# Moving a layout copy from VectorE to GpSimd, and logarithms ahead of sums, in a fused attention and feed-forward kernel

## Chip, cores and metric

The kernel runs on one core of one Trainium2 chip. The metric is the device time of one execution in microseconds (us), as a median of several runs. Engines are called by their names in the profile: PE (matmul), PEld (weight load), DVE (VectorE), ACT (ScalarE), POOL (GpSimd), SP (SyncE, which here only issues transfers). All times inside an execution count from the start of its span. L510 is line 510 of a kernel; the same line has other numbers in other kernels. A transfer *lands* when its data have arrived. The *granted clock* is the share of the full PE clock that the profile shows as granted. A run over 1.5% above the fastest of its kernel counts as slow, and ratios use fast runs alone.

## The reference, cut to what matters

```python
# q, k, v: 8 batches x 8 heads x 576 x 64;  s: 8 x 8 x 576;  all float32
scores = q @ k.transpose(0, 1, 3, 2) / sqrt(64)
cum    = cumsum(maximum(s, 0), axis=-1)
scores = where(causal, -1e9, scores + minimum(-(cum_i - cum_j), 0))   # (cut)
attn   = softmax(scores) ;  y = attn @ v
x      = y as 4608 tokens x 512
out    = gelu(x @ w_in) @ w_out        # w_in 512 x 2048, w_out 2048 x 512
```

The additive bias depends on the key through `cum_j`, so the kernel multiplies v and a row of ones by a weight per key (`wb`) instead of adding it to the scores. Attention is then, for each pair of heads, a numerator (P times weighted v) and a denominator (P times weights), and the quotient is formed as numerator times exp(−ln(denominator)).

## The kernel before

Tokens are worked in nine chunks of 512; chunk c runs the two feed-forward layers of its tokens on PE while the attention of batch c+1 is woven between them. Batch 0's attention is the prologue: nothing runs beside it. A batch has four pairs of heads, each with scores, an exponential (ACT), two mask products (DVE), the numerator and denominator (PE), a logarithm and an exponential (ACT) and the quotient `xT` (DVE). From batch 2 on, q and k are loaded with two heads apart, interleaved on chip (`interleave`), written to DRAM as rows and read back by transposing transfers. These are the pieces that the change touches:

```python
def interleave(b, n):                          # L176
    i = 0 if n == "q" else 1
    t = qk_of[b, i] = work.tile([128, 2, G, 2, D], bf16, tag="qkbf", bufs=2, name="qk_bf")
    for j in range(2):
        nc.vector.tensor_copy(                 # L180, DVE
            t[:, j].rearrange("g r e d -> g e r d"),
            early[b, n][:, j].rearrange("g e (r d) -> g e r d", r=G))

def av_banks(wide=False, last=False):          # PSUM for numerator and denominator
    if wide:
        t = ps.tile([128, 2, 512], fp32, tag="sc", bufs=2, name="avw")
        return t[:, 0], t[:, 1]                # both sums in ONE tile
    # ... otherwise two tiles, avn and avd

def av_item(b, p, wide=False, rest=True):
    num, den = av_banks(wide)
    av_mm(b, p, num, MAIN, False)              # L425, numerator first
    av_mm(b, p, den, MAIN, True)               # L425, then denominator
    if rest:
        av_rest(b, p)
    norm(b, p, p + 1, num, den, 0, CUT, [...]) # L442 ln, L443 exp (ACT), L458 xT (DVE)

# end of chunk 0, batch 1's attention between pieces of the second layer (cut)
            scale_pair(1, 2)                   # L232: v times weights, DVE
            av_item(1, 0, rest=False)
            scale_pair(1, 3)
            l2_item(c, 3, 8, 12)
            av_item(1, 1, wide=True, rest=False)
            interleave(2, "q")
            write_rows(2, 0, nc.sync)
            av_item(1, 2, wide=True, rest=False)
            l2_item(c, 3, 12)
            interleave(2, "k")
            write_rows(2, 1, nc.sync)
            av_item(1, 3, rest=False)
            # ... transposes of batch 2, loads of batch 3
```

## Time and profile before

| | before |
|---|---|
| median of 3 runs | 333.96 us (333.59 to 335.59) |
| profiled run | 333.42 us, span 331.6 us |
| PE busy | 317.4 us, 96% of the span |
| DVE, ACT, POOL busy | 191.3, 204.1, 66.0 us |
| chain that ended last | PE 81%, DMA 8%, ACT 4%, DVE 3% |
| prologue, chunks 0, 1, 2, 3 | 24.23, 38.32, 35.44, 35.21, 34.05 us |

PE is nearly always busy, so a change in another engine can only matter where PE stands still. The lines that show where it does stand in the prediction below, with how to read their columns.

### The profile page before, as it was taken

Reading aid. Unit: us, or ns where it says so; the run is one execution under the profiler, and the core shown is the slowest. Engines: PE = TensorE matmul, PEld = TensorE weight load, DVE = VectorE, ACT = ScalarE, POOL = GpSimd, SP = SyncE. Lnnn points to the kernel's source line nnn. Section 1 sums busy time; section 2 is a strip of 40 time slices with the busy share of each in tenths; the row PEclk is TensorE's granted clock in tenths of the full one; section 3 lists DMA queues with packets and bytes.
Section 4 is the critical chain, followed back from the end, with each engine's and each line's share of the span. In section 5 each row is a group of like instructions: output and inputs, shape, how many; then the busy total and the mean of one; then the engine's idle time right before and its main releaser. Section 6 shows DMA issues by size and latency. Waiting matters only on the chain.

```text
span 331.6 us, 8751 instructions
## 1 busy us (share of the span) xinstructions
PE 317.4 (96%) x3760; PEld 193.4 (58%) x3762; DVE 191.3 (58%) x382; ACT 204.1 (62%) x290; POOL 66.0 (20%) x100
## 2 busy tenths in 40 slices
PE   8879999999999999999999999999999999999992
PEld 3456645666666556656665566656665666555562
DVE  4659428997369464866577557845693764150021
ACT  3677656869567774767676777586768676204400
POOL 8754342002500370440035001300000000000000
PEclk9999999999999999999999999999999999999997
DMA  7999999564995699999759977625610110010012
GB/s 115 222 211 210 218 198 275 200 95 69 220 311 88 103 247 258 190 194 194 251 131 206 235 194 118 153 99 166 119 34 33 43 57 2 34 63 34 1 65 71
DMA packets 53838, 47.45 MB, mean 143 GB/s; under 512 B 31329, under 2 KB 43873, under 8 KB 53793
## 3 DMA queue, kind: packets, MB, share of 16 engines
q0 software_dynamic: 15936, 23.07, 38.0%
q1 hardware_dynamic: 37856, 23.75, 28.6%
q8 instruction: 31, 0.51, 0.6%
q14 instruction: 15, 0.11, 0.1%
HBM read 36.85 MB, written 16.52 MB: 161 GB/s over the span
## 4 chain that ended last, share of the span: by engine, by line
PE 81%; DMA 8%; ACT 4%; DVE 3%; issue 2%; POOL 1%; SPq 0%; DVEq 0%; POOLq 0%
PE h_ps L510 36%; PE o_ps L532 31%; DMA early_q<-in_q_dram 4%; PE sc_ps L387 4%; PE avd L425 3%; PE avn L425 3%; ACT P L403 2%; DMA qkT<-rows 2%; DVE xT L458 1%; PE o_ps L553 1%; DMA early_q<-in_k_dram 1%; PE tr_ps L366 1%; PE avr L425 1%; DVE qkT L372 1%; PE warm L582 1%
## 5 line engine op out<-in xcount | busy, mean ns | idle before, releaser
L532 PE MATMUL o_ps<-w_out_r,gT 128*64 128x512 bf16 x1120 | 129.8, 380 | 0.0
L510 PE MATMUL h_ps<-xT,w_in_r 128*64 128x512 bf16 x1152 | 126.4, 379 | 2.5 <-DVE xT L458 2.5
L510 PEld LDWEIGHTS <-w_in_r 128*64 128x64 bf16 x1152 | 76.5, 110 | 50.4 <-issue 3.3
L532 PEld LDWEIGHTS <-gT 128*64 128x64 bf16 x1120 | 62.7, 110 | 48.3
L517 ACT ACTIVATE gT<-h_ps 128x1024 bf16<-128x1024 f32 x54 | 54.3, 1022 | 49.9 <-PE h_ps L510 49.9
L403 ACT ACTIVATE P<-sc_ps 128x1024 bf16<-128x1024 f32 x64 | 62.0, 1021 | 30.8 <-PE sc_ps L387 27.2
L539 DVE COPY o_sb<-o_ps 128x512 f32<-128x512 f32 x35 | 24.0, 686 | 47.9 <-PE o_ps L532 47.9
L412 DVE TENSOR_TENSOR P<-P,tri_bf 128x512 bf16<-128x512 bf16 x58 | 24.0, 422 | 38.3 <-ACT P L403 38.0
L215 DVE TENSOR_REDUCE amx<-qkT 128x2 f32<-128x1152 bf16 x32 | 40.9, 1336 | 0.0
L204 POOL DMA_DIRECT2D raw_v<-in_v_dram x40 | 34.2, 879 | 9.5 <-DMA w_out_r<-in_moe_w_out_dram 4.8
L458 DVE SCALAR_TENSOR_TENSOR xT<-avn,ln 128x256 bf16<-128x256 f32 (+3 forms) x64 | 21.6, 384 | 22.3 <-ACT ln L443 22.2
L232 DVE TENSOR_TENSOR vv<-raw_v,wb 128x512 bf16<-128x512 f32 (+3 forms) x44 | 25.2, 632 | 0.0
L442 ACT ACTIVATE ln<-avd 128x256 f32<-128x256 f32 x56 | 18.6, 392 | 10.2 <-PE avd L425 10.2
L443 ACT ACTIVATE ln<-ln 128x512 f32<-128x512 f32 (+1 forms) x40 | 23.5, 588 | 1.3
L520 ACT ACTIVATE gT<-h_ps 128x512 bf16<-128x512 f32 x36 | 19.6, 603 | 6.3 <-PE h_ps L510 6.3
L387 PE MATMUL sc_ps<-qkT 64*128 64x256 bf16 (+2 forms) x320 | 21.1, 250 | 2.1 <-ACT P L403 1.0
L222 DVE TENSOR_REDUCE amv<-raw_v 128x1 f32<-128x2048 f32 (+1 forms) x16 | 22.9, 1470 | 0.0
L387 PEld LDWEIGHTS <-qkT 64*128 64x128 bf16 x320 | 12.9, 94 | 16.8 <-issue 12.2
L425 PEld LDWEIGHTS <-vv 128*64 128x64 bf16 x384 | 18.0, 110 | 4.9 <-PE sc_ps L387 0.9
L425 PEld LDWEIGHTS <-wb 128*64 128x64 bf16 x384 | 17.7, 111 | 1.8 <-issue 1.7
L425 PE MATMUL avd<-P,wb 128*64 128x256 bf16 x224 | 15.6, 260 | 1.0 <-DVE xT L458 1.0
L425 PE MATMUL avn<-P,vv 128*64 128x256 bf16 x224 | 15.8, 263 | 0.6 <-DVE P L412 0.6
(98 smaller groups left out, 156.9 us busy)
## 6 DMA issues: line engine op xcount, KB each, us to landing
out_dram<-o_sb SPq DMA_DIRECT2D x35, 256.0 KB, 3.2
raw_v<-in_v_dram POOLq DMA_DIRECT2D x32, 256.0 KB, 8.1
rows<-qk_bf SPq DMA_DIRECT2D x12, 576.0 KB, 6.1
early_q<-in_q_dram POOLq DMA_DIRECT2D x13, 288.0 KB, 10.6
early_k<-in_k_dram POOLq DMA_DIRECT2D x13, 288.0 KB, 11.7
w_in_r<-in_moe_w_in_dram POOLq DMA_DIRECT2D x4, 512.0 KB, 11.4
w_out_r<-in_moe_w_out_dram POOLq DMA_DIRECT2D x4, 512.0 KB, 14.3
raw_v<-in_v_dram POOLq DMA_DIRECT2D x8, 128.0 KB, 9.1
```

The costliest lines, as they stand in the source:

```text
L204: nc.gpsimd.dma_start(out=t[:n_st, st, :, :], in_=bass.AP(tensor=v.tensor, offset=v.offset + b * H * S * D + st * 128 * D, ap=[[D, n_st], ...
L215: nc.vector.tensor_reduce(amx[:, b * NP + p], qkT[b % 2][:, :, p, :S], axis=AX, op=ALU.max, apply_absolute_value=True)
L232: eng.tensor_tensor(vb[:n_st, st0:st1, h0:h1, :], t[:n_st, st0:st1, h0:h1, :], wb[:n_st, st0:st1, b * H + h0 : b * H + h1] .unsqueeze(3).t ...
L387: nc.tensor.matmul(s_ps[:, e, off : off + n], lhsT=qkT[b % 2][e * 64 : e * 64 + 64, 1, p, jt * 128 : jt * 128 + 128], rhs=qkT[b % 2][e * 6 ...
L403: nc.scalar.activation(P[:, :, UO[u] : UO[u] + UW[u]], s_ps[:, :, : UW[u]], func=AF.Exp, scale=scale)
L412: eng.tensor_tensor(d, d, tri_bf.unsqueeze(1).unsqueeze(1).to_broadcast([128, 2, 2, 128]), op=MULT)
L425: nc.tensor.matmul(out[e * 64 : e * 64 + 64, lo : lo + n], lhsT=(wb[:, jt, b * H + h : b * H + h + 1].to_broadcast([128, 64]) if den else ...
L458: nc.vector.scalar_tensor_tensor(out if p1 - p0 > 1 else out[:, 0], cut(num), math.exp(-LNC[c]), cut(ln), op0=MULT, op1=MULT,)
L510: nc.tensor.matmul(h_of[c, f2][i][e * 64 : e * 64 + 64], lhsT=w_in_r[:, ko, ft * 128 + e * 64 : ft * 128 + e * 64 + 64], rhs=xT[:, ko, c * ...
L517: nc.scalar.activation(gT_of[c][:, f2 * 2 : f2 * 2 + 2, :], hh_of[c, f2], func=AF.Gelu)
L532: nc.tensor.matmul(o_ps[e * 64 : e * 64 + 64], lhsT=gT[:, ft, t0 : t0 + 64], rhs=w_out_r[:, ft, :], start=(ft == 0), stop=(ft == FT - 1), ...
L539: nc.vector.tensor_copy(o_sb, o_ps)
```

## The change

Its intent is to shorten the places where PE waits: batch 0's scores are transposed and computed in the order in which the loads land (Part 1), the denominators and their logarithms come ahead of the numerators everywhere (Part 2), the end of chunk 0 is reordered and two copies move from DVE to ACT (Part 3), and the interleave goes from DVE to POOL for all batches (Part 4). The diff, cut to its core:

```diff
@@ interleave
-            nc.vector.tensor_copy(
+            nc.gpsimd.tensor_copy(
@@ norm is split: norm_act = ln and exp on ACT, norm_dve = the quotient on DVE
@@ av_item
     num, den = av_banks(wide)
+    av_mm(b, p, den, MAIN, True)
+    ln = norm_act(den, CUT, CHUNKS)
     av_mm(b, p, num, MAIN, False)
-    av_mm(b, p, den, MAIN, True)
     ...
-    norm(b, p, p + 1, num, den, 0, CUT, [(0, 0, 256), (1, 256, CUT)])
+    norm_dve(b, p, p + 1, num, ln, 0, CUT, CHUNKS)
@@ prologue (cut)
-    tr_items(0, 1, (0, 1))
-    weights_dve()
-    keep_busy(5)
+    keep_busy(1)
+    tr_items(0, 1, (0,))
+    keep_busy(2)
+    tr_items(0, 1, (1,))
+    keep_busy(3)
     sc_item(0, 1, neg=True, units=(0,))
     ...
+    lns = {p: norm_act(avs[p][1], CUT, CHUNKS) for p in (0, 1)}
     for p in range(NP):
         av_mm(0, p, avs[p][0], MAIN, False)
-        norm(0, p, p + 1, *avs[p], 0, CUT, [(0, 0, 256), (1, 256, CUT)])
+        norm_dve(0, p, p + 1, avs[p][0], lns[p], 0, CUT, CHUNKS)
+        if p + 2 < NP:
+            lns[p + 2] = norm_act(avs[p + 2][1], CUT, CHUNKS)
@@ chunk 0, after its first layer
             load_v(2)
+            interleave(2, "q")
+            interleave(2, "k")
@@ end of chunk 0 (cut)
+            av_item(1, 0, rest=False)
+            scale_pair(1, 2)
             l2_item(c, 3, 4, 8)
             sc_item(1, 3)
-            scale_pair(1, 2)
-            av_item(1, 0, rest=False)
+            av_item(1, 1, rest=False)
             scale_pair(1, 3)
+            write_rows(2, 0, nc.sync)
             l2_item(c, 3, 8, 12)
-            av_item(1, 1, wide=True, rest=False)
-            interleave(2, "q")
-            write_rows(2, 0, nc.sync)
             av_item(1, 2, wide=True, rest=False)
+            write_rows(2, 1, nc.sync)
             l2_item(c, 3, 12)
-            interleave(2, "k")
-            write_rows(2, 1, nc.sync)
             av_item(1, 3, rest=False)
```

More of the change, by code (lines that the diff above doesn't have):

```diff
@@ L436, with norm_act @@
     rest_of = {}
-    def norm(b, p0, p1, num, den, i0, i1, chunks):
+    def norm_act(den, w, chunks):
         ln = work.tile([128, CUT], fp32, tag="ln", bufs=2, name="ln")
-        w = (p1 - p0) * (i1 - i0)
         for c, lo, hi in chunks:
@@ L443, in norm, with norm_dve @@
         nc.scalar.activation(ln[:, :w], ln[:, :w], func=AF.Exp, scale=-1.0)
+        return ln
+    def norm_dve(b, p0, p1, num, ln, i0, i1, chunks):
+        w = (p1 - p0) * (i1 - i0)
         for c, lo, hi in chunks:
@@ L470, in av_banks @@
             return num, den
-        return [ps.tile([128, 512], fp32, tag="av", bufs=3, name=n) for n in ("avn", "avd")]
+        den, num = [ps.tile([128, 512], fp32, tag="av", bufs=3, name=n) for n in ("avd", "avn")]
+        return num, den
+    CHUNKS = [(0, 0, 256), (1, 256, CUT)]
     def av_item(b, p, wide=False, rest=True):
         num, den = av_banks(wide)
+        av_mm(b, p, den, MAIN, True)
+        ln = norm_act(den, CUT, CHUNKS)
         av_mm(b, p, num, MAIN, False)
-        av_mm(b, p, den, MAIN, True)
         if rest:
             av_rest(b, p)
-        norm(b, p, p + 1, num, den, 0, CUT, [(0, 0, 256), (1, 256, CUT)])
+        norm_dve(b, p, p + 1, num, ln, 0, CUT, CHUNKS)
     def av_rest(b, p):
@@ L488, in norm_rest @@
         t = rest_of[b].rearrange("d n p i -> d n (p i)")
-        norm(b, 0, NP, t[:, 0], t[:, 1], CUT, S, [(2, 0, NP * SL)])
+        chunks = [(2, 0, NP * SL)]
+        ln = norm_act(t[:, 1], NP * SL, chunks)
+        norm_dve(b, 0, NP, t[:, 0], ln, CUT, S, chunks)
     gT_of = {}
@@ L520, in l1_item, with l2_item @@
                 nc.scalar.activation(gT_of[c][:, f2 * 2 + i, :], h_of[c, f2][i], func=AF.Gelu)
-    def l2_item(c, sub, f0=0, f1=FT, av=False):
+    def l2_item(c, sub, f0=0, f1=FT, av=False, copy=None):
         gT = gT_of[c]
@@ L538, in l2_item @@
         o_sb = work.tile([128, KO * 128], fp32, tag="osb", bufs=3, name="o_sb")
-        nc.vector.tensor_copy(o_sb, o_ps)
+        (copy or nc.vector.tensor_copy)(o_sb, o_ps)
         r0 = c * NB + sub * 128
@@ L589 @@
     nc.vector.tensor_scalar(neg_bf, tri_bf, 2048.0, -2048.0, op0=MULT, op1=ALU.add)
+    keep_busy(1)
+    tr_items(0, 1, (0,))
+    keep_busy(2)
+    tr_items(0, 1, (1,))
     keep_busy(3)
-    tr_items(0, 1, (0, 1))
-    weights_dve()
-    keep_busy(5)
     sc_item(0, 1, neg=True, units=(0,))
     tr_items(0, 2, (0,))
+    keep_busy(1)
+    tr_items(0, 2, (1,))
+    weights_dve()
     sc_item(0, 1, neg=True, units=(1,))
+    tr_items(0, 3, (0,))
+    sc_item(0, 2, neg=True, units=(0,))
     weights_pe()
-    tr_items(0, 2, (1,))
+    tr_items(0, 3, (1,))
+    sc_item(0, 2, neg=True, units=(1,))
     mask_item(0, 0, 0, nc.vector)
-    tr_items(0, 3, (0,))
-    keep_busy(1)
-    sc_item(0, 2, neg=True)
-    tr_items(0, 3, (1,))
     mask_item(0, 0, 1, nc.vector)
@@ L671 @@
             l2_item(c, 1, 8, 12, av=True)
-            l2_item(c, 2, 0, 12, av=True)
-            l2_item(c, 0, 12)
+            l2_item(c, 2, 0, 8, av=True)
+            l2_item(c, 0, 12, copy=nc.scalar.copy)
+            l2_item(c, 1, 12, av=True)
             tr_items(1, 2, (0, 1), (nc.scalar.copy, nc.vector.tensor_copy), wide=True)
-            l2_item(c, 1, 12, av=True)
-            tr_items(1, 3, (0, 1), (nc.scalar.copy, nc.vector.tensor_copy), wide=True)
+            l2_item(c, 2, 8, 12, av=True)
+            tr_items(1, 3, (0, 1), (nc.scalar.copy, nc.scalar.copy), wide=True)
+            scale_pair(1, 0)
             l2_item(c, 2, 12, av=True)
-            scale_pair(1, 0)
+            scale_pair(1, 1)
             l2_item(c, 3, 0, 4)
             sc_item(1, 2)
-            scale_pair(1, 1)
+            av_item(1, 0, rest=False)
+            scale_pair(1, 2)
             l2_item(c, 3, 4, 8)
             sc_item(1, 3)
-            scale_pair(1, 2)
-            av_item(1, 0, rest=False)
+            av_item(1, 1, rest=False)
             scale_pair(1, 3)
+            write_rows(2, 0, nc.sync)
             l2_item(c, 3, 8, 12)
-            av_item(1, 1, wide=True, rest=False)
-            interleave(2, "q")
-            write_rows(2, 0, nc.sync)
             av_item(1, 2, wide=True, rest=False)
+            write_rows(2, 1, nc.sync)
             l2_item(c, 3, 12)
-            interleave(2, "k")
-            write_rows(2, 1, nc.sync)
             av_item(1, 3, rest=False)
```

## The prediction

> **What bounds the kernel now.** I read the page first: PE is busy 317.4 of 331.6 us and carries 81% of the chain that ended last. The question is therefore only where PE stands still and which of those places the change reaches. The busy times by stretch answer it. I cut at the first matmul of each chunk's first layer (L510) as the timeline gives it; the columns are length, busy time of PE, PEld, DVE, ACT and POOL (with instruction counts), granted clock, DMA share, GB/s.
>
> ```profile
> 0.00:24.23 24.23, 19.06 (x294) 10.88 (x296) 13.80 (x32) 14.11 (x22) 17.59 (x32) 1.00 1.04 180
> 24.23:62.55 38.32, 36.76 (x538) 22.57 (x538) 25.74 (x49) 27.23 (x41) 12.96 (x17) 1.00 1.06 207
> 62.55:97.99 35.44, 34.69 (x422) 22.80 (x423) 25.21 (x47) 23.81 (x35) 6.92 (x10) 1.00 0.84 190
> 97.99:133.20 35.21, 34.42 (x395) 21.82 (x392) 22.00 (x41) 24.05 (x35) 9.68 (x15) 1.00 0.87 179
> 133.20:167.25 34.05, 34.05 (x395) 20.69 (x392) 22.08 (x40) 23.95 (x35) 7.11 (x10) 1.00 1.04 201
> ```
>
> From 133.2 us on PE has no idle time (34.05 of 34.05; the next three stretches and the last full chunk are alike). No rearrangement of work on other engines can shorten these 200 us; it can only spoil them. The recoverable time lies in the prologue (24.23 us, of which 7.4 us are filler matmuls, L582), in chunk 0 (1.56 us idle), chunk 1 (0.75) and chunk 2 (0.79). The DMA share is about 1 up to 62 us: loads land when the queue gets to them, however early the compute is.
>
> The waits of PE, then the timeline, tell which work ends these gaps (start, length, instruction; in brackets the idle time before it and what ended it):
>
> ```profile
> PE h_ps L510 <- DVE xT L458: 2.5, 3, 1.1
> PE avd L425 <- DVE xT L458: 1.0, 2, 0.5
> PE avn L425 <- DVE P L412: 0.6, 2, 0.3
> ```
>
> ```profile
> 11.28 2.13 ACT L403 ACTIVATE P<-sc_ps 128x1024 bf16<-128x1024 f32 x2 [1.68 <-PE sc_ps L395]
> 14.81 1.94 ACT L403 ACTIVATE P<-sc_ps 128x1024 bf16<-128x1024 f32 x2 [1.03 <-PE sc_ps L395]
> 17.50 1.94 ACT L403 ACTIVATE P<-sc_ps 128x1024 bf16<-128x1024 f32 x2 [0.75 <-PE sc_ps L395]
> 20.86 0.66 ACT L442 ACTIVATE ln<-avw 128x256 f32<-128x256 f32 x2 [1.43 <-PE avw L425]
> 22.21 0.76 DVE L458 SCALAR_TENSOR_TENSOR xT<-avw,ln 128x256 bf16<-128x256 f32 x2 [2.45 <-ACT ln L443]
> 90.44 0.83 DVE L180 COPY qk_bf<-early_q 128x1152 bf16<-128x1152 bf16 x2 [3.74 <-DMA early_q<-in_q_dram]
> 120.51 1.01 DVE L180 COPY qk_bf<-early_q 128x1152 bf16<-128x1152 bf16 x2 [3.14 <-DMA early_q<-in_q_dram]
> ```
>
> In the prologue ACT sets the pace: four pairs of exponentials with 1.68, 1.03 and 0.75 us of idle time between them, then 1.43 us until the first logarithm, though its denominator was summed by about 19.2. At 90 and 120 us the in-order DVE stands 3.7 and 3.1 us before an interleave copy whose load has not landed; masks and xT products queue behind it, and PE waits for these (0.6 and 1.0 us of the wait list).
>
> **What the Trainium skill says.** "SBUF — State Buffer", section "SBUF: two separate sides": GpSimd shares a port pair with DVE as an exclusive lock held for a whole instruction; on the DVE side it concerns operations in a 2-port mode and, against a GpSimd operation that reads SBUF, those with two SBUF inputs. The trace agrees for one direction:
>
> ```profile
> 17.07 2.56 DVE L232 TENSOR_TENSOR vv<-raw_v,wb 128x512 bf16<-128x512 f32 x5
> 19.19 0.61 POOL L615 CAST pace<-w_in_r 128x1 f32<-128x1 bf16 x1 [4.54 <-DMA w_in_r<-in_moe_w_in_dram]
> 80.32 0.18 POOL L701 CAST pace<-qkT 128x1 f32<-128x1 bf16 x1 [27.48 <-DMA qkT<-rows]
> ```
>
> The one-column cast takes 0.18 us alone but 0.61 us when it starts inside the two-input products, ending just after their end at 19.63. Whether DVE waits in the same way for a long POOL copy no line shows yet. "GPSIMD Engine Reference", section "4.1 Engine selection", calls one-input GpSimd work roughly line rate. The trace has no long POOL copy, but memsets: 377 ns for 256 columns and 271 ns for 128, so 0.83 ns a column. My estimate for 1152 columns is 0.96 + 0.16 = 1.1 us a copy, with 1.9 us possible (section "3.1 Elementwise" of that page gives 1.8 cycles an element for a tight loop). On DVE it is:
>
> ```profile
> L180 DVE COPY qk_bf<-early_q 128x1152 bf16<-128x1152 bf16 x12 | 5.1, 467 | 6.9 <-DMA early_q<-in_q_dram 6.9
> L614 POOL MEMSET qkT<- 128x256 bf16 x1 | 0.4, 377 | 0.0
> L613 POOL MEMSET ones<- 128x128 f32 x1 | 0.3, 271 | 0.0
> ```
>
> **Part 1, chunk 0's scores in order of landing.** The loads of the four pairs land at 4.7/5.4, 7.6/8.3, 9.0/9.8 and 10.6/11.5 us (q/k, start plus time to landing), so transposing q and k of a pair apart lets the first qkT copy (0.75 us on DVE) start before k is there. Stepping the new order through with the old durations: pair 1's copies end at about 9.95 in place of 10.5, its exponentials start at 10.8 and 12.1 (before: 11.3, 12.3); pair 2's copies end at 12.5 since the 0.5 us subtraction of the weights (L260) moves behind them, exponentials at 13.35 and 14.85 with the two small weight exponentials between; pair 3's second copy ends at 14.85, exponentials at 15.8 and 16.75. The last ends at 17.7 instead of 19.44: 1.7 us. The V products (L232, 2.56 us) start after the masks at about 15.8 and end at 18.4; the last V load lands at 16.7, so it does not bind.
>
> **Part 2, logarithms ahead of the sums.** Before, L442 started 1.43 us after the last exponential, as it sat behind the numerator's sums. Now it can follow at once; the path becomes numerator of pair 0 at +1.3, xT of pair 0 at +2.05, of pair 1 at +3.25 us. Before, the continuous run of L510 began 24.23 − 19.44 = 4.8 us after the last exponential; now 3.25: 1.5 us. Together the prologue gives 1.7 + 1.5 = 3.2 us. The first w_in quarter lands at 19.14 and the others 2.6 us apart, ahead of use. In the later stages den-first moves logarithms 0.4 us earlier where nobody waits: 0.
>
> **Part 3, the end of chunk 0.** PE work there is unchanged; the copies move (an o_sb copy of 0.69 us and a qkT copy of 0.76 us from DVE to ACT). The V products of batch 1 now start at their landing (last V slice 50.45, set by the DMA queue) rather than at 53.6. Then PE follows DVE and ACT: four exponentials and two ln/exp pairs, 4 × 0.95 + 2 × 1.3 us, before the last V product on DVE. Stepped through, L510 of chunk 1 starts at about 58.9 against an effective 62.1: the prologue's 3.2 us are kept, nothing is added.
>
> **Part 4, the interleave on POOL.** In chunks 1 and 2 DVE no longer blocks, masks come some 2 us earlier, and PE's idle time goes: 0.75 + 0.79, with the stretched matmuls around them about 1.8 us (35.2 towards 34.05 in chunk 2, 0.7 of chunk 1's excess). On POOL the copies sit behind the issues of the next loads: batch 4's rows leave some 5 us later, at about +31 us of chunk 2, but its first scores come 15 us after that and the eight transposes take some 12 us, so it holds. From chunk 3 on the loads are a stage ahead and the copies run while DVE does one-input reductions: 0. But batch 2's four copies (4 × 1.1 us) start when q lands, at 54.2 us, and run to 59, exactly over the DVE chain of part 3: two V products, three masks, two more V products, all with two SBUF inputs. If the port blocks DVE as the page says, each pending one waits for a copy, 2 to 3.5 us in sum, and the gain of the prologue is mostly gone again by chunk 1.
>
> **The rivals.** (a) Quiet port: DVE does not wait; 333.96 − 3.2 − 1.8 = 329.0. Speaks for it: no line yet shows DVE waiting. (b) Blocked port: 2.8 us given back at chunk 0's end, 333.96 − 0.4 − 1.8 = 331.8. Speaks for it: the 0.61 us cast and the page. (c) The prologue is held by something I step over (V landing, PSUM slots): only 1.5 us of the 3.2 come, and the end of chunk 0, which waits for absolute landings anyway, absorbs them: 332 to 333. (d) Copies at 1.9 us each delay the rows of batch 2 or 4 and PE waits for scores: 333 or more; the margins of 5 us and more speak against it.
>
> **Range and chances.** I give (a) a third, (b) a half, the rest to (c) and (d): 0.33 × 329.0 + 0.5 × 331.8 + 0.17 × 332.5 = 331.0; as chunk 0's own 1.56 us of idle time may shrink more than I stepped out, I take 330.6. The low end 327.8 is (a) with 1.2 us of that idle time; the high end 333.0 is (c). Faster by 2% means under 327.3, a saving of 6.7 us: it needs nearly all of the prologue's 3.2, chunk 0's 1.6 and the 1.8. I give it 0.08; slower by 2% would need a new wait in every stage, 0.02.
>
> **What would show it.** Right: last prologue exponential ends near 17.7; first logarithm directly after it; the run of L510 starts near 21.0; no DVE wait for early loads; 34.1 us in chunk 2; POOL copies of 1.1 to 1.9 us; V products or masks stretched beyond 0.68 and 0.42 us between 54 and 60 us (rival b) or not (rival a). Wrong: any new idle time of PE after 133 us, transposes landing after PE wants them, or a prologue no shorter than 23 us.

## The result and the profile after

The kernel after takes 330.53 us (median of 6 runs, 330.33 to 331.91). The kernel before took 334.22 us in its 6 runs beside it (333.07 to 335.59). The ratio is 0.9895 with a 95% interval of 0.9866 to 0.9924: about 1% faster, within the 2% that count as the same. A ratio is the mean time of one kernel's fast runs over that of the other's of the same rounds, so it is not quite the ratio of the medians. The profile is of the slowest of the six (331.91 us).

The busy times by stretch, cut as in the prediction at the start of each chunk's uninterrupted first layer (now L519; starts as the chain view gives them, where no wait stands before it some 0.2 us later than in the timeline), show at once where time came from and where it went:

```profile
0.00:21.42 21.42, 18.17 (x290) 10.98 (x294) 14.30 (x32) 13.96 (x22) 16.04 (x31) 1.00 1.02 180
21.42:62.00 40.58, 37.13 (x541) 22.88 (x538) 27.20 (x46) 29.55 (x44) 19.07 (x23) 1.00 1.12 223
62.00:96.42 34.42, 34.40 (x422) 22.16 (x423) 24.53 (x42) 23.03 (x35) 11.53 (x14) 1.00 0.88 191
96.42:130.47 34.05, 34.05 (x395) 19.36 (x392) 22.56 (x37) 23.88 (x35) 13.92 (x19) 1.00 0.88 184
130.47:165.70 35.23, 34.12 (x394) 19.53 (x392) 20.76 (x36) 23.94 (x35) 11.65 (x14) 1.00 1.09 179
```

| stage | before, us | after, us | difference |
|---|---|---|---|
| prologue | 24.23 | 21.42 | −2.81 |
| chunk 0 | 38.32 | 40.58 | +2.26 |
| chunk 1 | 35.44 | 34.42 | −1.02 |
| chunk 2 | 35.21 | 34.05 | −1.16 |
| chunk 3 | 34.05 | 35.23 | +1.18 |
| the rest | 164.35 | 164.30 | −0.05 |

The sum is −1.60 us, which is the difference of the two spans (331.6 and 330.0). Four fifths of what the prologue gained went in chunk 0, and a new 1.2 us appeared in chunk 3. A repeat of this kernel (e5_after_again below) took 39.76 us for chunk 0 and 34.06 us for chunk 3, so both figures vary from run to run.

**Prologue.** ACT's timeline after (start, length, instruction): the last exponential ends at 15.35 + 2.92 = 18.27 us, and the first logarithm follows at once, where before it stood idle for 1.43 us.

```profile
15.35 2.92 ACT L403 ACTIVATE P<-sc_ps 128x1024 bf16<-128x1024 f32 x3 [0.28 <-PE sc_ps L395]
18.16 0.66 ACT L441 ACTIVATE ln<-avw 128x256 f32<-128x256 f32 x2
```

**End of chunk 0.** The timeline of DVE and POOL after, cut to the rows that changed: POOL's four interleave copies of batch 2 run from 56.08 to 61.15 us, and DVE's masks (L412, L417) and V products (L232) between those times take 1.73, 1.16 and 2.11 us.

```profile
55.77 1.73 DVE L412 TENSOR_TENSOR P<-P,tri_bf 128x512 bf16<-128x512 bf16 x2
56.08 2.43 POOL L180 COPY qk_bf<-early_q 128x1152 bf16<-128x1152 bf16 x2 [3.68 <-DMA early_q<-in_q_dram]
57.42 1.16 DVE L417 TENSOR_TENSOR P<-P,tri_bf 128x128 bf16<-128x128 bf16 x1
58.45 2.70 POOL L180 COPY qk_bf<-early_k 128x1152 bf16<-128x1152 bf16 x2
59.17 2.11 DVE L232 TENSOR_TENSOR vv<-raw_v,wb 128x512 bf16<-128x512 f32 x2
```

Without a copy beside them the same rows take 0.78, 0.22 and 0.87 us (the run e1_late below), so 0.95 + 0.94 + 1.24 = 3.1 us of DVE time are waiting. (Each row is one pair of masks, one small mask, and one V product of 512 columns with its small remainder.)

**What PE waits for.** The wait list of the kernel after (us in total, times, longest us) has the xT wait down from 2.5 to 0.8 us, and none of before's waits for masks; new are a logarithm, a V product and transposed rows:

```profile
PE avw L425 <- ACT ln L441: 2.3, 2, 1.9
...
PE sc_ps L387 <- DMA qkT<-rows: 1.1, 1, 1.1
```

PE's timeline after places them: 1.88 us before the numerator at 57.90 (chunk 0's end), and 1.11 us before scores at 159.70 (chunk 3).

```profile
57.90 0.57 PE L425 MATMUL avw<-P,vv 128*64 128x256 bf16 x8 [1.88 <-ACT ln L441]
...
159.70 0.61 PE L387 MATMUL sc_ps<-qkT 64*128 64x256 bf16 x10 [1.11 <-DMA qkT<-rows]
```

The first is a numerator that writes one half of the shared tile `avw` while the logarithm still has to read the other half, the denominator. Before, the numerator went first and nothing read the tile yet.

The groups of instructions of the kernel after, kept apart by shape (busy time, mean ns), give the price of the copies on POOL, 1.2 us each where DVE took 0.46 to 0.47:

```profile
L180 POOL COPY qk_bf<-early_k 128x1152 bf16<-128x1152 bf16 x12 | 14.2, 1227 | 0.0
L180 POOL COPY qk_bf<-early_q 128x1152 bf16<-128x1152 bf16 x12 | 13.8, 1197 | 4.8 <-DMA early_q<-in_q_dram 3.7 <-issue 1.1
```

### The profile page after: what moved, and what is told of

Read it like the earlier page. It is cut to its first block, busy times and chain, and to the rows that moved or that the text cites. A ratio compares the mean times of both kernels' runs of the same rounds, so it can differ in the third digit from the quotient of the medians.

```text
span 330.0 us, 8736 instructions
## 1 busy us (share of the span) xinstructions
PE 316.3 (96%) x3757; PEld 183.6 (56%) x3760; DVE 189.2 (57%) x356; ACT 204.9 (62%) x292; POOL 93.1 (28%) x124
## 4 chain that ended last, share of the span: by engine, by line
PE 85%; DMA 6%; ACT 2%; DVE 2%; issue 1%; SPq 0%; POOL 0%; DVEq 0%; POOLq 0%
PE h_ps L519 37%; PE o_ps L541 33%; DMA qkT<-rows 5%; PE sc_ps L387 5%; PE avd L425 3%; PE avn L425 3%; PE tr_ps L366 1%; ACT P L403 1%; DMA early_q<-in_k_dram 1%; PE o_ps L562 1%; PE avr L425 1%; DVE vv L232 1%; ACT ln L441 1%; DVE xT L461 0%; DVE qkT L372 0%
## 5 line engine op out<-in xcount | busy, mean ns | idle before, releaser
L519 PE MATMUL h_ps<-xT,w_in_r 128*64 128x512 bf16 x1152 | 126.2, 379 | 0.8 <-DVE xT L461 0.8
L519 PEld LDWEIGHTS <-w_in_r 128*64 128x64 bf16 x1152 | 68.4, 110 | 56.6 <-issue 1.3
L541 PEld LDWEIGHTS <-gT 128*64 128x64 bf16 x1120 | 61.3, 110 | 49.4
L412 DVE TENSOR_TENSOR P<-P,tri_bf 128x512 bf16<-128x512 bf16 x58 | 28.2, 491 | 47.8 <-ACT P L403 47.1
L461 DVE SCALAR_TENSOR_TENSOR xT<-avn,ln 128x256 bf16<-128x256 f32 (+3 forms) x66 | 22.4, 386 | 21.0 <-ACT ln L442 14.4
L232 DVE TENSOR_TENSOR vv<-raw_v,wb 128x512 bf16<-128x512 f32 (+3 forms) x44 | 26.6, 662 | 0.3 <-DMA raw_v<-in_v_dram 0.3
L442 ACT ACTIVATE ln<-ln 128x512 f32<-128x512 f32 (+1 forms) x40 | 23.5, 587 | 1.3
L665 POOL CAST pace<-gT 128x1 f32<-128x1 bf16 x4 | 1.9, 485 | 57.6 <-ACT gT L526 57.6
L425 PE MATMUL avd<-P,wb 128*64 128x256 bf16 x232 | 16.8, 264 | 0.0
```

The costliest lines, as they stand in the source:

```text
L232: eng.tensor_tensor(vb[:n_st, st0:st1, h0:h1, :], t[:n_st, st0:st1, h0:h1, :], wb[:n_st, st0:st1, b * H + h0 : b * H + h1] .unsqueeze(3).t ...
L412: eng.tensor_tensor(d, d, tri_bf.unsqueeze(1).unsqueeze(1).to_broadcast([128, 2, 2, 128]), op=MULT)
L425: nc.tensor.matmul(out[e * 64 : e * 64 + 64, lo : lo + n], lhsT=(wb[:, jt, b * H + h : b * H + h + 1].to_broadcast([128, 64]) if den else ...
L442: nc.scalar.activation(ln[:, :w], ln[:, :w], func=AF.Exp, scale=-1.0)
L519: nc.tensor.matmul(h_of[c, f2][i][e * 64 : e * 64 + 64], lhsT=w_in_r[:, ko, ft * 128 + e * 64 : ft * 128 + e * 64 + 64], rhs=xT[:, ko, c * ...
L541: nc.tensor.matmul(o_ps[e * 64 : e * 64 + 64], lhsT=gT[:, ft, t0 : t0 + 64], rhs=w_out_r[:, ft, :], start=(ft == 0), stop=(ft == FT - 1), ...
```

## The experiments

Twelve kernels ran, in four groups. The first four (chip 7) shared runs of the kernel before with a median of 335.41 us (one of 7 slow). The next four (chip 9) had 334.31 us, e9 to e11 (chip 9) 333.96 us, e12 (chip 2) 333.84 us. Each ratio is to the kernel before of the same group. Where an interval lies above 1 and reaches across 1.02, the kernel is slower than before, but whether by the 2% that count is unclear.

**Theory.** Chunk 0's end lost the prologue's gain because POOL's copies hold the port that DVE's two-input products need, and because the logarithm now stands ahead of the numerator in a shared tile. Chunk 3's wait comes from rows that leave late. **Rivals.** The prologue's gain is lost anyway, since loads land at fixed times; the tile wait or the port alone explains it; the late rows are only traffic of the moment.

### The parts alone: e4_order_only and e3_pool_only

e4_order_only is the kernel before with the prologue's order of Part 1 alone:

```diff
-    tr_items(0, 1, (0, 1))
-    weights_dve()
-    keep_busy(5)
+    keep_busy(1)
+    tr_items(0, 1, (0,))
+    keep_busy(2)
+    tr_items(0, 1, (1,))
+    keep_busy(3)
     # ... and so on for pairs 2 and 3, as in the change
```

> The kernel before, with only the prologue's scores in order of landing. If this part is worth what the changed kernel's trace shows: last exponential of the prologue ends near 18.3 instead of 19.4 us, first layer of chunk 0 runs on from about 23.1 instead of 24.2, and, as chunk 0's end follows PE and not a landing here, the total falls by 1.0 to 1.2 us. Rival (absolute landings of batch 1 absorb it): the total is unchanged within 0.3 us.

Measured: 340.18 us (338.52 to 341.08), ratio 1.0151 [1.0078, 1.0223]: slower than before, whether by 2% unclear, and neither expectation had such a loss. The first matmul of each chunk's first layer shows why (before in brackets): chunk 0 at 21.80 (23.12), chunk 1 at 59.94 (61.24), chunk 2 at 97.34 (97.80), chunk 3 at 133.07 (133.02), chunk 4 at 173.85 (167.06). The 1.3 us of the prologue reach chunk 1 whole. They are gone two chunks later, because the q load of batch 3 lands at 89.90 us (90.36 in before), hardly earlier: DVE stands in front of its interleave copy until then, masks queue behind it, and PE waits the longer the earlier it comes (1.07 us at 91.29 us for a mask). In chunk 3 PE then waited for a transpose of batch 4 that landed at 161.40 us (the same one in before: 154.17); the last one landed at 162.52 us (159.43 in before). PE's timeline of this run:

```profile
161.44 1.04 PE L387 MATMUL sc_ps<-qkT 64*128 64x256 bf16 x10 [5.07 <-DMA qkT<-rows]
```

Most of the transposes were issued within 1 us of before's times, the last 5 us later. Why the transfers served them later is not settled by this trace. What follows is that the prologue's gain by itself is absorbed by loads that land at fixed times (those of batches 3 and 4, not of batch 1 as the rival had it), and that chunk 3 sits close to an edge.

e3_pool_only is the kernel before with the interleave on POOL, one word of the diff:

```diff
-            nc.vector.tensor_copy(
+            nc.gpsimd.tensor_copy(
```

> The kernel before, with the interleave on POOL and nothing else. Port theory: chunks 1 and 2 lose their 2.2 us (35.44 and 35.21 towards 34.4 and 34.05), but chunk 0's end pays 1 to 2.5 us as POOL copies run from 54 to 59 us over its masks and V products; total 0 to 1.2 us under the kernel before. Rival (DVE does not wait for the port): 2.2 us less, chunk 0 unchanged at 38.3 us.

Measured: 343.08 us (340.80 to 345.04), ratio 1.0236 [1.0147, 1.0326]: slower than before, whether by 2% unclear. At chunk 0's end the port costs more here than in the full change, since before's order has more two-input work left at 55 us: a V product with its remainder took 2.24 us and a pair of masks 2.63 us beside POOL's copies. PE's timeline:

```profile
62.25 0.81 PE L425 MATMUL avw<-P,vv 128*64 128x256 bf16 x8 [2.09 <-DVE vv L232]
```

Chunk 1 began at 66.35 us in place of 62.55, and around it the granted clock was 0.61 and 0.53 for 4 us. Of these 3.8 us some 1.5 were lost before any copy ran: between 24 and 28 us the granted clock was 0.73 and 0.50 (1.00 in the first profile of before), and chunk 0's first layer took 15.47 us in place of 13.83; e11_before_profile shows the same 15.47 us in the unchanged kernel. Chunk 2 has a wait again (1.60 us), behind a single mask that took 5.11 us beside four POOL copies. The largest loss is in chunk 3, which took 39.7 us with waits of 0.94 and 3.00 us for transposed rows. So Part 4 alone loses 2.4%, Part 1 alone 1.5%, and all parts together win 1%. The parts are not a sum. My reading, which no run shows by itself: with the interleave off DVE, chunks 1 and 2 of the kernel after no longer wait for early loads, and this lets the prologue's gain survive.

### The end of chunk 0: e1_late, e2_wide and e7_both

e1_late takes the port collision away: batch 2's copies start only when the last V product is done.

```diff
-            interleave(2, "q")      # ahead of chunk 0's second layer
-            interleave(2, "k")
...
             scale_pair(1, 3)
+            nc.gpsimd.tensor_copy(pace, vv[1][:, 0, 7, 0:1])
+            interleave(2, "q")
+            interleave(2, "k")
             write_rows(2, 0, nc.sync)
```

> The changed kernel, but batch 2's four POOL copies wait (by a one-column POOL cast that reads the last V product of batch 1) until chunk 0's last two-input DVE operation is done. Port theory: masks and V products between 55 and 60 us fall back to 0.42 and 0.68 us each (changed kernel: two masks 1.73, the small mask 1.16, two V products 2.11 us), the last V product ends near 59 instead of 61.3, chunk 1's first layer runs on from about 60.0 instead of 61.6: 1.6 us less up to there. Rival (the 1.9 us wait of PE for the logarithm in the shared wide PSUM tile is the only bound): less than 0.6 us. In both, rows of batch 2 leave 2 to 3 us later, so a longer wait for transposes in chunk 3 can take some of it back; total 328.5 to 330.5 us.

Measured: 339.24 us (336.11 to 342.97, one slow), ratio 1.0065 [0.9977, 1.0152]. The collision was gone, yet chunk 1 began at 61.65 us: chunk 0, from first matmul to first matmul of the first layer, took 40.32 us, no less than in the kernel after (60.60 − 21.23 = 39.37, and another 0.8 us of waiting four matmuls later). First the timeline of DVE and PE, then the busy times by stretch of this run:

```profile
55.87 0.78 DVE L412 TENSOR_TENSOR P<-P,tri_bf 128x512 bf16<-128x512 bf16 x2
...
57.99 0.96 PE L425 MATMUL avw<-P,vv 128*64 128x256 bf16 x8 [2.09 <-ACT ln L441]
58.10 0.87 DVE L232 TENSOR_TENSOR vv<-raw_v,wb 128x512 bf16<-128x512 f32 x2
```

```profile
58.00:60.00 2.00, 2.00 (x15) 1.40 (x16) 1.73 (x5) 0.60 (x1) 1.07 (x2) 0.50 0.47 141
```

DVE finished its last V product at 58.97 us in place of 61.28, so the port's effect is shown by taking it away. But PE still waited 2.09 us for the logarithm in the shared tile: between 55 and 58 us ACT was busy 2.94 of 3.00 us, so the logarithm came late. After the wait PE ran at half its clock (0.50 in the stretch above, 0.65 in the next 2 us; eight second-layer matmuls took 1.96 us, 1.03 elsewhere). Rows of batch 2 left 2 to 3 us later, and in chunk 3 PE waited 5.78 us for transposes.

e2_wide takes the tile wait away instead: for the one item with a shared tile the numerator goes ahead of the logarithm.

```diff
     av_mm(b, p, den, MAIN, True)
+    if wide:
+        av_mm(b, p, num, MAIN, False)
     ln = norm_act(den, CUT, CHUNKS)
-    av_mm(b, p, num, MAIN, False)
+    if not wide:
+        av_mm(b, p, num, MAIN, False)
```

> The changed kernel, but in the one item whose sums share a wide PSUM tile (batch 1, pair 2) the numerator is summed before the logarithm reads the tile. Tile theory: the 1.9 us wait of PE before that numerator goes. Port theory: the last V product still ends near 61.3 us under the POOL copies, so chunk 1 starts at most 0.3 us earlier and the total stays within 0.3 us of the changed kernel. If the tile were the bound: 1.5 to 1.9 us less.

Measured: 332.40 us (331.61 to 333.22), ratio 0.9917 [0.9854, 0.9979]. The wait at 57.9 us disappeared and another took its place. The timeline of DVE and PE:

```profile
59.24 2.57 DVE L232 TENSOR_TENSOR vv<-raw_v,wb 128x512 bf16<-128x512 f32 x2
60.71 0.61 PEld L425 LDWEIGHTS <-vv 128*64 128x64 bf16 x8 [2.96 <-DVE vv L232]
60.71 0.96 PE L425 MATMUL avn<-P,vv 128*64 128x256 bf16 x8 [2.74 <-ACT ln L442]
```

The matmul's row names L442, which works in SBUF alone and ended at 60.72 by chance. What this numerator needs is the V product, as the row of its weight load says: the first and larger of the two instructions in the DVE row took 1.42 us of the 2.57, stretched by the POOL copies, and ended at 60.66, when the wait ended. The granted clock was then 0.50 from 60 to 66 us, and chunk 0 took 61.46 − 21.33 = 40.13 us.

e7_both takes both away.

> Run e1 and run e2 in one kernel: batch 2's POOL copies after the last V product of batch 1, and numerator before logarithm in the shared wide tile. Theory of two parallel bounds (each alone hid behind the other): no PE wait over 0.7 us between 55 and 60 us, no drop of the granted clock there, and chunk 1's first layer runs on from 59.2 to 59.7 us, against 61.6 in each alone: 2 us. Rival (a third bound, ACT's logarithms): 60.5 or later. Total is not the measure here, as later rows can make chunk 3 wait.

Measured: chunk 1 began at 59.64 us, 2 us earlier than with either edit alone, with one wait of 0.65 us at chunk 0's end and no lower clock. PE's timeline:

```profile
59.23 0.57 PE L425 MATMUL avn<-P,vv 128*64 128x256 bf16 x8 [0.65 <-DVE vv L232]
```

Chunk 0 took 59.64 − 21.51 = 38.13 us, against 40.32 and 40.13 (38.12 in before, by the same measure). So port and shared tile are two bounds side by side: each makes PE wait when the other is gone (2.09 and 2.74 us). What each costs is less sure, since in e1 and e2 half clock adds to the loss. From that numerator to chunk 1's first layer e1 took 3.66 us, and e9_qk_behind below, with the same order and full clock, 2.02; so some 1.6 us of e1's loss are the clock's, and e9 itself took 38.84 us with both bounds in place. The median was all the same 338.43 us (337.03 to 340.40), ratio 1.0158 [1.0109, 1.0208], because batch 2's rows left at 61.7 and 63.9 us (58.8 and 61.5 in a repeat of the kernel after), the next loads followed late, and batch 3's POOL copies now fell at 89.9 to 94.7 us onto the masks of chunk 1 (a pair of masks took 2.68 us), those of batch 4 onto the masks of chunk 2 (4.83 us). PE waited 1.44, 1.91 and 2.39 us in chunks 1 to 3, which took 36.3, 36.8 and 38.2 us.

### Chunk 3's wait: e5_after_again, e6_pace, e9_qk_behind and e11_before_profile

e5_after_again is the kernel after, unchanged, beside e6 to e8.

> The changed kernel once more, as a control beside the next runs on one chip. Its recorded gain (ratio 0.9895) should come back within 0.5%. Theory of the late transposes: in its profile the last transposes of batch 4 land within 2 us of the moment PE wants them in chunk 3 (recorded run: 1.1 us late, kernel before: 1.8 us early), so its runs scatter by the wait that follows; rival: the 1.1 us was a single accident and chunk 3 takes 34.05 us here.

Measured: 331.25 us (329.75 to 333.38), ratio 0.9945 [0.9897, 0.9993]. Its profile (of the run of 329.75 us) shows the tile wait again, 1.88 us at 57.89, but less of the port: q landed at 56.40 us in place of 56.02, DVE was through with the masks (0.78 and 0.22 us), and only the V product was stretched, to 2.46 us, so 1.6 us in place of 3.1. The tile wait is the steadier of the two. Chunk 3 took 34.05 us: batch 4's last transpose landed at 156.89 us and PE asked for it at 157.7. In the first profile it landed at 159.66 and PE asked at 158.6. So the wait of chunk 3 comes and goes with a landing that varies by some 3 us.

e11_before_profile is the kernel before, profiled once more.

> The kernel before, unchanged, as a profile on this chip. It shows how near batch 4's transposes land to the first scores of chunk 3 there. The prediction named a margin of 5 us and more; the first profile had 1.8 us (landed 159.43, wanted 161.25). If the margin is a property of the kernel before and not of that one run, it is again 1 to 3 us, and chunk 3 takes 34.05 us; if it was chance, it is 5 us or more.

Measured: one run of 338.24 us, the slowest of this kernel, so of unknown state; it is not used for times. The landing came at 160.83 us, the use at 166.2: a margin of 5.4 us, but only because PE was 5 us later by then, 3 of them from chunk 2, which took 38.18 us. Measured from the start of the run, the landing lies within 1.4 us in the two profiles of this kernel (159.43 and 160.83 us). The run is of use for another thing. In chunk 2 it had the wait that Part 4 removes, longer than in the first profile. First PE's timeline, then the busy times by stretch after it:

```profile
125.27 0.60 PE L425 MATMUL avn<-P,vv 128*64 128x256 bf16 x8 [1.62 <-DVE P L412]
```

```profile
127.00:129.00 2.00, 2.00 (x13) 1.13 (x13) 2.00 (x7) 1.21 (x3) 0.61 (x1) 0.57 1.05 222
```

Waits of 1.62 and 0.44 us were followed by 4 us at a granted clock of 0.57 and 0.58, and the chunk lost 4.1 us in all, twice the waits.

e6_pace issues the loads from chunk 3 on only after the next batch's transposes have landed.

```diff
         if 1 < c and nb + 1 < B:
             nc.gpsimd.tensor_copy(pace, gT_of[c][:, 0, 0:1])
+            nc.gpsimd.tensor_copy(pace, qkT[nb % 2][:, 1, 3, 0:1])
             load_v(nb + 1)
```

> The changed kernel, but from chunk 3 on the loads of the batches ahead are issued only after the transposes of the next batch have landed (one more one-column POOL cast that reads the last qkT tile). If the loads ahead of them in the DMA rings make the transposes late: batch 4's transposes land 8 to 15 us earlier (near 145 in place of 159.7 us), chunk 3 takes 34.05 us in every run, the runs scatter less, total 328.5 to 329.5 us on an undisturbed chip, 1 to 6 us under the control where that waits. Rival (the writes of the rows are what is late): the landing moves by less than 3 us.

Measured: 333.87 us (332.49 to 334.10), ratio 0.9991 [0.9949, 1.0032]. Batch 4's transposes landed at 144.91 us, 12 us earlier than in e5, and chunk 3 took 34.05: the late landing is shown to depend on when the next loads are issued. But the loads, now later, pushed POOL's copies (queued behind their issue) onto chunk 4's masks. DVE and POOL timeline:

```profile
184.03 5.39 DVE L412 TENSOR_TENSOR P<-P,tri_bf 128x512 bf16<-128x512 bf16 x2
184.65 2.32 POOL L180 COPY qk_bf<-early_q 128x1152 bf16<-128x1152 bf16 x2
```

A pair of masks took 5.39 us; the second of them alone took 4.71 us (0.42 without copies), until all four copies were done, and chunk 4 took 36.8 us. One thing the port of the copies does not explain: at 182.32 us a small mask took 1.18 us (0.22 elsewhere) while POOL ran no copy and only issued loads. Its cause is open. The port that was free there in the kernel after is free only by timing.

e9_qk_behind moves just one issue: in chunk 2, batch 5's q and k loads go behind batch 4's copies in POOL's queue.

```diff
-            if nb + 2 < B:
+            if nb + 2 < B and c > 2:
                 load_qk(nb + 2)
...
                     interleave(nb + 1, "k")
                     write_rows(nb + 1, 1, nc.sync)
+                    if c == 2:
+                        load_qk(nb + 2)
```

> The kernel after, with one edit: in chunk 2 the issue of batch 5's q and k loads is moved behind batch 4's interleave copies in the order of the POOL queue; nothing else moves. Theory (the transposes of batch 4 hang on rows that leave late, since the copies stand in the POOL queue behind the next loads, and the rows then share the DMA queue with those loads): batch 4's rows leave earlier, its last transposes land by about 152 us of the profiled run instead of 157 to 160, chunk 3 takes 34.05 us in the profile whatever the run, and the median is the same as or up to 1 us below the kernel after (329.5 to 331.5), with less scatter. Rival (the late landing is only DMA traffic of the moment, and the order on POOL does not matter): landing stays at 157 to 160 us and a wait of about 1 us in chunk 3 is seen again. Second rival (the move takes the loads of batch 5 too late): chunk 4 gets a wait for them.

Measured: 329.99 us (329.58 to 334.80, one of six slow), ratio 0.9892 [0.9858, 0.9926]. The last transpose landed at 153.79 us (expected: about 152), and chunk 3 took 34.05. The copies themselves ran no earlier than in e5 (118.50 to 123.3 us against 117.76 to 122.2). So the expected path, rows leaving earlier, is wrong; what is left is that batch 5's loads were issued later (123.25 to 125.09 us in place of 113.68 to 117.15), and this fits e6_pace. The median is 1.3 us below e5's, in another round on the same chip, so this edit by itself is not shown to be faster than the kernel after. Chunk 0, unchanged, took only 38.84 us here, with q landing at 56.78 and 1.1 us of the port: how much the port costs is a matter of when a load lands.

### Towards a better kernel: e8_best, e10_best2 and e12_dve2

e8_best is e7_both with the line of e6_pace.

> Run e7 with the pacing of run e6: if chunk 0's end and chunk 3's wait are independent, the total is e6's less 2 us, 326.5 to 327.5 us on an undisturbed chip; if the later rows of batch 2 cost as much elsewhere (chunk 1 or 2 waiting for loads or scores), it is at e6's or above.

Measured: runs of 329.94 and 339.58 to 340.35 us. Three of its four runs lie over 1.5% above its fastest and so count as slow, and there is no ratio. The profile is of a slow run and has PE waits of 1.22, 0.94, 2.22, 1.13, 1.96 and 0.87 us in several chunks. I draw no conclusion from it but that it isn't better.

e10_best2 is e7_both with the edit of e9_qk_behind, and the loads of batches 3 and 4 released by an earlier transpose.

> An attempt to beat both kernels: the kernel after, with (1) batch 2's interleave behind the last V product of chunk 0, so that the shared port is free there, (2) the numerator ahead of the logarithm for the one item whose two sums share a PSUM tile, (3) batch 5's q and k loads issued behind batch 4's interleave as in the run before, and (4) the loads of batches 3 and 4 released by the transposes of pair 1 rather than pair 3. If port and shared tile are the two parallel bounds of chunk 0's end, and the late rows are what spoiled the earlier try of (1)+(2): chunk 1 starts at 59.4 to 59.8 us, chunks 1 and 2 take 34.0 to 34.6 us, chunk 3 34.05 us, and the median is 326 to 328. Rival: taking (1) pushes batch 2's rows and so every later transpose and copy back; whatever chunk 0 gains returns as waits for qkT in chunks 1 to 3 and as half-clock stretches after them, and the median is 331 or more.

Measured: 333.16 us (331.26 to 333.83), ratio 0.9977 [0.9943, 1.0011]. The first layer of chunk 1 began at 58.82 us, but PE waited 2.08 us at 89.78 for transposed rows, and chunks 1 and 2 took 36.9 and 35.4 us. The rival's number came, but not by its path: batch 2's last transpose was issued no later than in e7_both (74.51 us, there 75.28) and landed 10 us later (89.74, there 79.61). What differs is that batch 3's loads were released earlier, at 72.74 us in place of 80.18. So the fourth edit is the likelier cause, as e6_pace suggests; the edits were not separated.

e12_dve2 gives the port up: batch 2's interleave alone goes back to DVE, in the gaps behind V product and quotient. With it come the edits of e2_wide and e9_qk_behind.

```diff
             scale_pair(1, 3)
+            interleave(2, "q", nc.vector.tensor_copy)
             write_rows(2, 0, nc.sync)
             l2_item(c, 3, 8, 12)
             av_item(1, 2, wide=True, rest=False)
+            interleave(2, "k", nc.vector.tensor_copy)
             write_rows(2, 1, nc.sync)
```

> The second attempt to beat both kernels: the kernel after, with (1) batch 2's interleave alone back on DVE, the q copies behind the second V-scaled pair's xT product and the k copies behind the third's, as in the kernel before; (2) the numerator ahead of the logarithm for the one item whose sums share a PSUM tile; (3) batch 5's q and k loads behind batch 4's interleave, as in the run that did this alone. Batches 3 to 6 stay on POOL. Theory (at chunk 0's end the two bounds are the port held by POOL's copies and the shared tile; rows must not leave later than 59 to 62 us): no DVE instruction of 53 to 60 us is stretched (masks 0.8 us a pair, V products 0.9 us), rows leave at about 60 and 62 us, chunk 1 starts at 59.5 to 60.5 us in place of 61.3 to 62.0, chunks 1 to 3 take 34.05 to 35.3 us each as before this edit, and the median is 328.5 to 329.7, some 1 us under the run with (3) alone. Rival: DVE is itself full at chunk 0's end, its 1.6 us of copies delay the xT products by as much as the port did, and chunk 1 starts at 61 us or later: 330 to 331.5.

Measured: 329.04 us (328.83 to 330.85, 6 runs), ratio 0.9863 [0.9824, 0.9902]. The timeline of DVE and PE at chunk 0's end:

```profile
58.29 0.88 DVE L232 TENSOR_TENSOR vv<-raw_v,wb 128x512 bf16<-128x512 f32 x2
59.02 0.57 PE L425 MATMUL avn<-P,vv 128*64 128x256 bf16 x8 [0.94 <-DVE vv L232]
59.09 0.81 DVE L180 COPY qk_bf<-early_q 128x1152 bf16<-128x1152 bf16 x2
60.62 5.59 PE L522 MATMUL h_ps<-xT,w_in_r 128*64 128x512 bf16 x50 [0.59 <-DVE xT L461]
```

No two-input product is stretched, the uninterrupted first layer begins at 60.62 us (a little later than the 59.5 to 60.5 expected), rows leave at 59.9 and 61.3 us, batch 4's transposes land at 151.62 us against a use at 157.2, and the granted clock is 1.00 from 57 to 95 us. It has the lowest median of all kernels run, 1.4% below the kernel before. Its three edits were not separated. Against the kernel after (ratio 0.9895 in other rounds) the intervals overlap, so its lead over that is not settled. The profiles point the same way: from chunk 0's first matmul to chunk 2's it takes 73.43 us, the kernel after 75.02 and 74.21 (e5), e9 74.21.

## Why the prediction was right

The predicted time was 330.6 us, the measured median 330.53, within the range and the predicted class. The terms of the sum, from the two profiles:

| step of the prediction | predicted, us | measured, us |
|---|---|---|
| Part 1: last exponential ends earlier | −1.7 | 19.44 − 18.27: −1.17 |
| Part 2: first layer follows sooner | −1.5 | 4.79 − 3.15: −1.64 |
| prologue in all | −3.2 | −2.81 |
| chunk 0 with a blocked port (rival b) | +2.8 | +2.26 in one profile, +1.44 in another |
| Part 4, chunks 1 and 2 | −1.8 | −1.02 − 1.16: −2.18 |
| Part 4, chunk 3 | 0 | +1.18 in one profile, 0 in another |

Starting from the profiled run of before, 333.42 − 2.81 + 2.26 − 2.18 = 330.69 us: without chunk 3's wait the terms come close to the median. The repeat agrees: with its chunk 0 (+1.44) they give 329.87 us, and its profiled run took 329.75.

**That the point was hit within 0.1 us is luck.** 330.6 is the number of no rival: it is the weighted mean, 331.0, less 0.4 because chunk 0's idle time "may shrink more than I stepped out". The rival that came true stood at 331.8, and chunk 0's idle time did not shrink but grew, from 1.56 to 3.45 us (40.58 − 37.13). A smaller loss in chunk 0, a larger gain in chunks 1 and 2 and a lower base (333.42 us, the profiled run, where the prediction took the median 333.96) make up the difference.

**The prologue** was stepped through rightly, with Part 1 sized half a microsecond too high and Part 2 hit. e4_order_only confirms Part 1 by itself (−1.3 us at chunk 0).

**Rival (b) is what happened.** DVE waits for POOL's copies, 3.1 us in sum where "2 to 3.5 us" stood (1.6 in the repeat), and e1_late shows it by removing them. The share of one half given to it, against one third for (a), was the right way round. But (b) was told as the only thing that could take the gain back. "Stepped through, L510 of chunk 1 starts at about 58.9" and "nothing is added" do not hold even with a free port: e1_late waited 2.09 us for a logarithm. With both waits out of the way it started at 59.64 us (e7_both) and 58.82 (e10_best2), so the stepping was right but for them. Nor does "each pending one waits for a copy" hold everywhere: in e6_pace one mask waited for four. The failed term is Part 2's "in the later stages den-first moves logarithms 0.4 us earlier where nobody waits: 0". Where both sums share a tile somebody does wait: the numerator, 1.88 us at chunk 0's end and 0.42 in the prologue (the 2.3 of the wait list). The line `return t[:, 0], t[:, 1]` was there to be read. As the two waits lie side by side (e1_late, e2_wide, e7_both), the loss came out near rival (b)'s 2.8 us with only one of them in it, which is luck too.

**Part 4** in chunks 1 and 2 went as predicted and gave a little more, 2.2 in place of 1.8 us, and the copies took 1.2 us for an estimated 1.1. The estimate was drawn from two memsets of different types (256 columns of bf16, 128 of float32), so that it came this near is partly luck.

**The margin was mis-sized.** "Its first scores come 15 us after that and the eight transposes take some 12 us, so it holds", and against rival (d) "the margins of 5 us and more speak against it". In the kernel before, the last transpose landed at 159.43 and PE asked at 161.25: a margin of 1.8 us, to be read in the profile that I had. The term that was wrong is the 12 us: from the first issue, at 131.85, the eight took 27.6 us there. The rows themselves did not leave 5 us later, as stepped out, but at 120.98 and 123.14 us (before: 121.55 and 124.47). A shift of the use by 3 us earlier, which the change itself was to bring, was bound to test it. It cost 1.11 us in the profiled run and nothing in the repeat, so the median hardly shows it. The prediction named "transposes landing after PE wants them" as a sign of its being wrong, and in the profiled run this sign is there.

**What the prediction had not at all** is that its parts depend on one another: it priced each by itself and added. Part 1 alone (+1.5%) and Part 4 alone (+2.4%) are each slower than before. The sum was right only for the whole.

## What to carry to other kernels

Where the bounding engine is nearly full, look at absolute landing times first: work moved earlier is kept only if what it meets next comes earlier too. Before an elementwise copy goes to POOL, list the two-input DVE products that can fall beside it, in every stage and not only where it now runs. When a read of a sum is moved ahead of a second sum, check whether both are halves of one PSUM tile.

## What the Trainium skill lacked or had wrong

- "SBUF — State Buffer", section "SBUF: two separate sides", has the exclusive port right for these runs, and its direction that no line of before showed is now shown: DVE products with two SBUF inputs wait for POOL copies (masks 1.73 for 0.78 us, and one mask 4.71 for 0.42 us beside four copies). Quotients with one PSUM input beside the copies were not stretched (0.74 us for two), which fits its wording.
- "GPSIMD Engine Reference", section "4.1 Engine selection", calls one-input work roughly line rate. For choosing an engine a number is missing: the bf16 copy of 1152 columns took 1.2 us on POOL and 0.46 to 0.47 us on DVE, 2.6 times as long.
- "TensorE: Matmul & The Clock Gate", section "What's actually happening", has the clock fall after at least one idle window of about 3.4 us. Here waits of 2.09 us (e1_late) and of 1.62 and 0.44 us (e11_before_profile) were followed by some 4 us at granted clocks of 0.50 to 0.65, while 1.88 us (after) and 2.08 us (e10_best2) were not. Waits of 1.14 and 0.71 us at 23 to 24 us were followed by 0.73 and 0.50 in e3_pool_only, and waits of 1.14 and 0.70 us there by 1.00 in the first profile of before. So shorter waits can do it, and not always. The page calls the window free-running, which may be why; no run here shows that.
- No page that I found says that a sum into one half of a PSUM tile whose halves are 512 float32 columns each may have to wait for the read of the other half; in this program it did, for 1.88 us, and reversing the order took the wait away (e2_wide). Whether the chip asks for this wait or the program's own tracking of dependencies, no run here shows.
